# A long convolution and a token-mixing MLP on one core: zeros on TensorE ahead of the data, a third w2 buffer, a new order

## The chip, the cores and the metric

The kernel runs on one core of one Trainium2 chip. The metric is the device time of the whole program in microseconds, the median of several runs, lower is better. Five engines work side by side from their own instruction streams: TensorE (PE, matmul), VectorE (DVE), ScalarE (ACT), GpSimd (POOL) and SyncE (SP), which here only starts DMAs. They are tied together by semaphores.

## The reference, cut to what matters

There are S = 2048 tokens, D = 640 channels and F = 1536 hidden units, in bf16. The input `q` is also the input `x` of the second branch.

```python
def _A_ref(q, k, v, shift_k, ssm_k, ssm_D):        # causal long convolution
    k_shift[t] = sum_j k[t - j] * shift_k[:, j]     # 4 taps (written shorter here)
    kv = k_shift * v
    y = irfft(rfft(pad(kv, 2 * S)) * rfft(pad(ssm_k, 2 * S)))[:S].astype(bfloat16)
    y = y + kv * ssm_D
    return q * y

def _B_ref(x, w1, b1, w2, b2):                      # MLP over the tokens
    h = _layernorm(x)                               # over D
    u = gelu(einsum("bsd,sf->bdf", h, w1) + b1)
    return transpose(einsum("bdf,fs->bds", u, w2) + b2)

g = sigmoid((x * gate_w).sum(-1))
return g * a + (1 - g) * b
```

## The kernel before

**The convolution** is done in P = 4 blocks of 512 rows. A block of the filter `ssm_k` comes in as `wnat`, DVE folds it into sums and differences (`en`), the folds are transposed to `eo`, and TensorE multiplies `eo` by the tables `TFc` and `TFs` of cosines and sines, which gives the spectrum W. For blocks 0 and 1 the transposes are matmuls with the identity `idp`, and ACT copies them from PSUM to `eo`; for blocks 2 and 3 they are DMA transposes (`w_turn`, `w_freq`). A block of keys comes in transposed as `kT`, TensorE applies the 4 taps (`dg`), ACT copies the result to `ks`, a DMA transposes it to `kn`, DVE multiplies it by `vn` and folds it to `es` and `fs` (`kv_block`), and TensorE multiplies these by `AFc` and `AFs`; ACT writes the spectrum A (`a_freq`). DVE then forms the products of A and W block by block into `tT` and Z (`pair`), TensorE goes back with the table `TI` (`inverse`), and the `epilogue` takes `pb` and `qb` from PSUM on ACT, combines them in `cg` on DVE, multiplies them by the gated inputs `xe` and adds them to the output, mostly by accumulating DMAs of POOL. The last frequency needs its own small operation: the rows `nr0` to `nr3` are copied by four small DMAs into `WN`, a sum over neighbours gives `WN2`, and DVE multiplies it by `AN` into `ZN`.

**The MLP**: DVE makes the layernorm (`bn_stats`, then `h`), TensorE multiplies `h` by `w1` in groups of rows, ACT applies gelu into `gT`. Then `mlp2(q)` runs eight times: it loads 256 columns of `w2` (768 KB) and multiplies them in two groups of 24 matmuls of 320 columns, and ACT writes `o1`. The loads of w2 take turns in two buffers:

```python
        def w2_load(q):
            nm = f"w2_{q % 2}"
            dma(b[nm][:, :, :], dram(B_w2, q * 256, [[S, 128], [128 * S, FT], [1, 256]]), nm, 40.0 + q)
```

**What sets the order.** The program is first collected as a list of some 730 operations (`_Plan`). The tuple `ORDER` (lines 329 to 362) is a permutation of their numbers, and `plan.run(ORDER)` issues them in that order, each on its engine; so every engine's stream follows `ORDER`. A tracker adds a semaphore wait wherever an operation reads or overwrites what another engine or DMA produced. PSUM has four slots, given to the operations in the same order; buffers in SBUF are placed by their lifetimes. All DMAs but the gathering and accumulating ones are started by SP, in order, and a DMA that has to wait on SP holds those behind it.

**Names in the profile.** Each kind of operation is issued by one helper, so its line is the helper's: L310 matmul, L659 tensor-tensor, L666 and L667 tensor-scalar, L674 copy, L701 activation, L278 DMA, L265 DMA transpose, L269 to L273 POOL's DMAs, L677 memset, L884 and L886 layernorm statistics. Groups are told apart by the tile names.

Of the kernel before, what the change touches and what calls it, by code (L numbers as in the profile page):

```python
# [8 lines left out]
BF16 = mybir.dt.bfloat16  # L9
# [309 lines left out]
def bass_gated_mix__ssm_conv_h3__mixer_token_mlp__prompt_kernel(  # L319
# [7 lines left out]


ORDER = (
    12, 9, 13, 11, 14, 10, 21, 22, 155, 26, 15, 5, 0, 24, 23, 27, 1, 203, 28, 204, 16, 25, 31, 217, 32, 156, 205,  # L330
    206, 208, 160, 207, 154, 30, 209, 210, 332, 17, 18, 43, 44, 153, 211, 162, 166, 169, 40, 42, 41, 212, 213, 159,
    171, 38, 65, 161, 218, 214, 215, 216, 37, 58, 172, 219, 67, 33, 174, 36, 72, 6, 177, 59, 175, 170, 176, 220, 221,
    77, 29, 66, 3, 4, 73, 228, 34, 178, 35, 57, 2, 167, 68, 163, 164, 173, 232, 76, 229, 83, 74, 94, 75, 183, 78,
    116, 179, 105, 60, 168, 84, 39, 184, 61, 19, 20, 185, 180, 181, 234, 182, 107, 87, 88, 89, 106, 190, 233, 62,
    333, 95, 120, 138, 49, 150, 69, 109, 149, 151, 186, 235, 236, 99, 198, 191, 85, 192, 187, 63, 64, 199, 226, 227,
    127, 193, 335, 152, 86, 117, 118, 96, 200, 201, 97, 202, 79, 196, 121, 122, 80, 81, 98, 100, 197, 290, 108, 336,
    224, 82, 90, 194, 195, 188, 91, 119, 225, 230, 337, 70, 189, 71, 158, 132, 101, 231, 341, 92, 339, 342, 110, 340,
    279, 280, 281, 102, 222, 123, 103, 124, 104, 338, 343, 93, 140, 129, 334, 111, 112, 344, 282, 143, 223, 128, 130,
    139, 131, 133, 295, 142, 157, 46, 50, 113, 144, 45, 141, 114, 115, 47, 48, 283, 125, 126, 134, 135, 284, 136,
    285, 145, 137, 52, 54, 286, 146, 148, 259, 260, 147, 291, 287, 258, 409, 292, 408, 345, 346, 51, 53, 288, 289,  # L340
    407, 238, 237, 261, 239, 240, 352, 298, 356, 296, 357, 347, 353, 348, 349, 364, 360, 361, 297, 365, 562, 293,
    294, 7, 354, 355, 367, 358, 350, 359, 362, 363, 270, 351, 264, 265, 262, 268, 266, 263, 561, 271, 269, 274, 563,
    165, 243, 267, 368, 241, 244, 247, 242, 248, 245, 246, 253, 254, 564, 275, 276, 277, 272, 273, 423, 251, 252,
    413, 255, 256, 299, 366, 249, 250, 330, 331, 373, 257, 410, 278, 411, 374, 375, 369, 376, 371, 370, 429, 372,
    402, 404, 406, 303, 378, 401, 403, 405, 377, 412, 300, 304, 305, 56, 426, 590, 55, 427, 428, 430, 301, 560, 302,
    431, 414, 415, 591, 306, 565, 432, 379, 425, 380, 390, 381, 391, 383, 384, 385, 388, 389, 382, 392, 393, 592,
    396, 593, 418, 397, 596, 597, 307, 314, 433, 569, 398, 399, 567, 578, 566, 577, 579, 394, 386, 387, 311, 467,
    395, 416, 417, 598, 312, 313, 424, 580, 419, 420, 600, 568, 581, 469, 421, 308, 422, 309, 582, 434, 315, 319,
    310, 475, 599, 624, 322, 476, 625, 435, 626, 473, 471, 472, 400, 468, 474, 316, 317, 327, 436, 320, 457, 437,
    318, 458, 627, 323, 470, 594, 328, 628, 584, 459, 629, 460, 461, 478, 477, 329, 438, 446, 321, 442, 324, 447,  # L350
    325, 595, 440, 443, 326, 441, 452, 453, 454, 455, 603, 630, 479, 462, 614, 439, 481, 448, 449, 444, 445, 583,
    480, 486, 601, 487, 632, 631, 482, 463, 464, 602, 613, 604, 518, 465, 512, 466, 501, 636, 498, 499, 502, 503,
    450, 483, 519, 451, 504, 511, 505, 637, 456, 488, 506, 520, 638, 490, 572, 491, 605, 633, 616, 521, 615, 492,
    522, 570, 507, 575, 640, 493, 639, 508, 530, 515, 664, 571, 513, 665, 489, 634, 509, 573, 531, 524, 514, 8, 510,
    576, 500, 533, 574, 496, 532, 516, 666, 484, 485, 534, 525, 588, 606, 527, 667, 585, 517, 523, 542, 497, 668,
    635, 611, 608, 528, 607, 610, 543, 669, 617, 589, 609, 526, 670, 621, 612, 672, 671, 678, 535, 673, 545, 641,
    546, 587, 645, 618, 536, 529, 554, 656, 586, 674, 648, 647, 622, 675, 679, 494, 643, 654, 644, 677, 544, 547,
    623, 646, 676, 642, 653, 655, 537, 657, 682, 619, 539, 652, 650, 538, 658, 555, 683, 540, 495, 651, 548, 680,
    557, 684, 681, 686, 620, 556, 688, 541, 558, 702, 551, 552, 687, 649, 559, 705, 703, 685, 689, 690, 692, 693,
    659, 691, 694, 695, 661, 660, 697, 696, 708, 662, 698, 699, 709, 710, 700, 718, 549, 711, 717, 553, 707, 719,  # L360
    720, 713, 701, 704, 663, 712, 722, 714, 721, 550, 706, 715, 716, 723, 724, 725,
)


# [123 lines left out]
def _build(nc, A_q, A_k, A_v, A_shift_k, A_ssm_k, A_ssm_D, B_x, B_w1, B_b1, B_w2, B_b2, gate_w, out):  # L488
# [9 lines left out]
    FT = F // 128  # L498
# [5 lines left out]
    with ExitStack() as es:  # L504
# [15 lines left out]
        def buf(name, shape, dtype, t0, t1):  # L520
            spec.append((name, list(shape), dtype, t0, t1))

        END = 999
        buf("WN", [128, P + 1, 8], BF16, 0, END)
        buf("WN2", [128, P, 8], BF16, 0, END)
        buf("AN", [128, P, 8], BF16, 0, END)
        buf("ZN", [128, P, 8], BF16, 0, END)
        buf("PT", [128, P, 8], F32, 0, END)
        buf("gwc", [128, DC, 32], BF16, 0, 91)
# [7 lines left out]
        buf("nmr", [128, NT], F32, 0, 40)  # L537
        buf("gpre", [128, NT], F32, 0, END)
        buf("gth", [128, NT], F32, 0, END)
# [62 lines left out]
            buf(f"A{j}", [128, 2, NB, D], BF16, (50, 62, 82, 86)[j], END)  # L602
        for i in range(2):
            buf(f"Z{i}", [128, 2, NB, D], BF16, (62, 64)[i], END)
            buf(f"w2_{i}", [128, FT, 256], BF16, 91, END)
        NO = NT // 2
        WTD = (2, 3)
# [43 lines left out]
        def nel(ap):  # L651
            k = 1
            for st, ct in list(ap.ap)[1:]:
                k *= ct
            return k
# [20 lines left out]
        def memset(ap, val, pr, eng="POOL"):  # L676
            return vop(eng, 0.3 + nel(ap) / 2000.0, lambda e: e.memset(ap, val), [], [ap], pr)  # L677
# [40 lines left out]
        def pe(pslist, mms, pr, after=()):  # L718
            reads = []
            for m in mms:  # L720
                reads.append(m[3])
                reads.append(m[4])
            cost = sum(0.025 if len(m) == 8 else 0.035 if len(m) > 7 else max(0.1, 0.0235 + m[2] * 0.000375 + (0.02 if m[2] > 400 else 0))
                       for m in mms)

            def emit():
                full = []
                for m in mms:
                    ps_ = pp[m[0].slot]
                    if len(m) == 8:  # L730
                        o_ = ps_[m[7]:m[7] + 32, m[1]:m[1] + m[2]]
                    elif len(m) > 7:
                        q0, h0, z0 = m[7:]
                        o_ = ps_[q0:q0 + 64, h0:h0 + 512].rearrange("p (k z) -> p k z", k=2)[:, :, z0:z0 + 128]
                    else:
                        o_ = ps_[0:list(m[3].ap)[-1][1], m[1]:m[1] + m[2]]
                    full.append((o_,) + m[3:7])
                T.mm_part(full)

            return plan.add("PE", cost, emit, reads, [], pr, ps=pslist, after=after)  # L740
# [7 lines left out]
        def h2(ap):  # L748
            return ap.rearrange("p (c f) -> p c f", c=2)

        b = bufs
        cst = b["cst"]

        memset(cst[:, 0:1], float(np.float32(math.pi * (1.0 - 1e-6))), 0)
        memset(cst[:, 1:2], float(np.float32(-math.pi / 2)), 0)
# [106 lines left out]
        def w1t(s_, t):  # L862
            return b[f"w1_{(2 * s_ + t // 8) % 3}"][:, t % 8, :]
# [50 lines left out]
        p_ = _PS()  # L914
# [95 lines left out]
        for s_ in range(1, NSET):  # L1010
            w1_load(s_, 2.5 if s_ < 2 else 6.0 + 2 * s_)
            for fi in range(FSET):
                p_ = _PS(True)
                for hf in range(2):
                    pairs = [(w1t(s_, t)[:, fi * 128:(fi + 1) * 128], b["h"][:, t, :]) for t in range(8 * hf, 8 * hf + 8)]
# [147 lines left out]
                    dma(row5(Z, 7 * D), b["ZN"][:, m_, 0:5], f"zn{m_ % 2}", pr)  # L1163

        def w2_load(q):
            nm = f"w2_{q % 2}"
            dma(b[nm][:, :, :], dram(B_w2, q * 256, [[S, 128], [128 * S, FT], [1, 256]]), nm, 40.0 + q)

        def mlp2(q):
            w2_load(q)  # L1170
            for k in range(2):
                sb = 2 * q + k
                p_ = _PS()
                pairs = [(b[f"w2_{q % 2}"][:, ft, k * 128:(k + 1) * 128], b["gT"][:, ft, :]) for ft in range(FT)]
                pe([p_], halves(p_, pairs), 50.0 + q)
                act(h2(b[f"o1_{q}"][:, k, :]), two(p_), ACT.Identity, 3, bias=b["c2"][:, sb:sb + 1],
                    scale=b["omg"][:, sb:sb + 1], ps=[p_])
            if q < NO - 2:
                dma(rows(out, q), b[f"o1_{q}"][:, :, :], f"o1_{q}", 1.5)
            else:  # L1180
                dma(rows1(out, 2 * q + 1), b[f"o1_{q}"][:, 1, :], f"o1_{q}", 1.5)
# [103 lines left out]
        p_ = _PS()  # L1285
# [43 lines left out]
```

## Time and profile before

| | us |
|---|---|
| median of 3 runs | 190.94 (190.90 to 191.12) |
| the profiled execution's own time | 190.03 |
| span of the profile, first to last instruction | 188.0 |
| TensorE busy | 175.3 |
| DVE busy | 175.2 |
| ACT busy | 112.6 |
| POOL busy | 65.1 |

The span is 2.0 us shorter than the time of the same execution; the median of the runs is 0.91 us above that execution. Busy times of engines overlap, so they don't add up to the span; a group's mean is the duration of one record, and consecutive matmuls overlap, so that their pitch is shorter than a record.

### The profile page before, as it was taken

What the parts mean: (1) busy time and instruction counts of PE and PEld (TensorE: products, weight loads), DVE (VectorE), ACT (ScalarE), POOL (GpSimd) and SP (SyncE); (2) the same over time, 40 slices, a digit from 0 to 9 for tenths busy, and PEclk for the clock granted to TensorE, in tenths of its full rate; (3) what the DMA queues carried; (4) which work ended last, traced back from release to release, by engine and by line L of the source; (5) the groups of instructions that cost most, each with busy time, mean ns of one, the idle gap of its engine ahead of it and who ended that gap; (6) DMA issues with size and microseconds to landing.
All of it is one profiled execution on the core that took longest, in us unless ns stands there. A gap on an engine that the chain in (4) does not pass through costs nothing.

```text
span 188.0 us, 3972 instructions
## 1 busy us (share of the span) xinstructions
PE 175.3 (93%) x1636; PEld 124.1 (66%) x1636; DVE 175.2 (93%) x216; ACT 112.6 (60%) x173; POOL 65.1 (35%) x84
## 2 busy tenths in 40 slices
PE   0899999999999999999999999999999999996980
PEld 0566776766668766677776767677777777774750
DVE  6889999976999999999999999999999999999863
ACT  5989978439997079523420588453742845561781
POOL 7125587730000012000000000260068829988470
PEclk9999999999999999999999999999999999999997
DMA  5999989999999999994967892025688997598796
GB/s 164 315 266 277 338 235 247 228 125 201 289 232 231 193 233 228 257 242 119 247 190 145 185 277 73 2 71 170 168 246 274 209 247 229 107 185 241 128 148 130
DMA packets 78094, 38.04 MB, mean 202 GB/s; under 512 B 42492, under 2 KB 77564, under 8 KB 78076
## 3 DMA queue, kind: packets, MB, share of 16 engines
q1 hardware_dynamic: 75340, 32.87, 70.9%
q0 software_dynamic: 2736, 4.92, 14.3%
q8 instruction: 13, 0.21, 0.4%
q14 instruction: 5, 0.04, 0.1%
HBM read 23.08 MB, written 4.92 MB: 149 GB/s over the span
## 4 chain that ended last, share of the span: by engine, by line
PE 89%; DMA 7%; DVE 1%; ACT 0%; ACTq 0%; SPq 0%; issue 0%
PE pp L310 89%; DMA w<-in_B_w_dram 4%; DMA wnat<-in_A_ssm_k_dram 2%; DVE cg L659 1%; ACT o L701 0%; ACTq L322 0%; DVE en L659 0%; SPq L278 0%
## 5 line engine op out<-in xcount | busy, mean ns | idle before, releaser
L310 PE MATMUL pp<-gT,w 128*128 128x320 bf16 x384 | 53.4, 299 | 1.6 <-DMA w<-in_B_w_dram 1.6
L310 PE MATMUL pp<-h,w 128*128 128x320 bf16 x384 | 54.2, 299 | 0.1
L310 PEld LDWEIGHTS pp<-gT,w 128*128 128x128 bf16 x384 | 37.4, 98 | 16.4 <-DMA w<-in_B_w_dram 1.9
L659 DVE TENSOR_TENSOR tT<-A,W 128x5120 bf16<-128x5120 bf16 (+2 forms) x18 | 45.5, 2525 | 2.8 <-ACT A L701 2.6
L310 PEld LDWEIGHTS pp<-h,w 128*128 128x128 bf16 x384 | 36.9, 98 | 15.5 <-issue 1.3
L659 DVE TENSOR_TENSOR Z<-Z,tT 128x2560 bf16<-128x2560 bf16 (+5 forms) x29 | 46.4, 1625 | 0.1
L271 POOL DMA_INDIRECT xe<-in_A_q_dram,bidx x8 | 20.6, 2575 | 66.3 <-PE pp L310 48.7
L701 ACT ACTIVATE o<-pp,c,omg 128x640 bf16<-128x640 f32 x16 | 13.9, 881 | 21.7 <-PE pp L310 21.7
L701 ACT ACTIVATE A<-pp 128x640 bf16<-128x640 f32 x32 | 20.7, 712 | 7.8 <-PE pp L310 7.7
L271 POOL DMA_INDIRECT vn<-in_A_v_dram,bidx x8 | 9.4, 1170 | 32.5 <-DVE kn L659 31.4
L701 ACT ACTIVATE gT<-pp,bf 128x640 bf16<-128x640 f32 x12 | 9.3, 793 | 16.6 <-PE pp L310 16.6
L310 PE MATMUL pp<-Z,TI 128*128 128x320 bf16 x128 | 18.9, 299 | 0.0
L269 POOL DMA_INDIRECT out_dram<-cg,bidx x8 | 15.5, 1936 | 2.9 <-issue 1.8
L701 ACT ACTIVATE W<-pp 128x640 bf16<-128x640 f32 x24 | 15.6, 759 | 1.0 <-PE pp L310 1.0
L310 PEld LDWEIGHTS pp<-Z,TI 128*128 128x128 bf16 x128 | 12.2, 98 | 5.2 <-ACT o L701 0.2
L884 DVE BATCH_NORM_STATS2 stats<-xs 128x6 f32<-128x320 bf16 x32 | 13.8, 471 | 0.1
L310 PE MATMUL pp<-eo,TFc 128*128 128x320 bf16 x64 | 12.6, 321 | 0.0
L701 ACT ACTIVATE ks<-pp 128x1024 bf16<-128x1024 f32 (+1 forms) x12 | 10.1, 892 | 3.6 <-PE pp L310 3.6
L659 DVE TENSOR_TENSOR Z<-A,W 128x5120 bf16<-128x5120 bf16 x4 | 11.3, 2822 | 0.5 <-ACT A L701 0.5
L310 PE MATMUL pp<-eo,TFs 128*128 128x320 bf16 x64 | 10.5, 300 | 0.0
L310 PE MATMUL pp<-idp,en 128*128 128x128 bf16 x40 | 4.7, 287 | 5.6 <-DVE par_i L666 4.7
L310 PE MATMUL pp<-kT,dg 64*64 64x256 bf16 x320 | 9.8, 270 | 0.0
(100 smaller groups left out, 207.5 us busy)
## 6 DMA issues: line engine op xcount, KB each, us to landing
w<-in_B_w_dram SPq DMA_DIRECT2D x8, 768.0 KB, 5.8
w<-in_B_w_dram SPq DMA_DIRECT2D x10, 512.0 KB, 4.7
xs<-in_A_q_dram SPq DMA_DIRECT2D x7, 320.0 KB, 5.1
out_dram<-o SPq DMA_DIRECT2D x6, 320.0 KB, 4.8
vn<-in_A_v_dram SPq DMA_DIRECT2D x4, 320.0 KB, 3.8
wnat<-in_A_ssm_k_dram SPq DMA_DIRECT2D x2, 640.0 KB, 6.2
xe<-in_A_q_dram SPq DMA_DIRECT2D x4, 320.0 KB, 3.1
w<-in_B_w_dram SPq DMA_DIRECT2D x4, 256.0 KB, 5.2
```

The lines of the kernel that those rows point to most:

```text
L269: ins = engobj.indirect_dma_start(whole, off, in_ap, None, compute_op=ALU.add)
L271: ins = engobj.indirect_dma_start(out_ap, None, whole, off)
L310: ins = self.nc.tensor.matmul(ps_ap, lhsT=lhsT, rhs=rhs, start=start, stop=stop)
L659: return vop(eng, c, lambda e: e.tensor_tensor(out_, in0, in1, op), [in0, in1], [out_], pr)
L701: return e.activation(out_, src, func, **kw)
L884: vop("DVE", 0.41, (lambda o_, i_: lambda e: e.bn_stats(o_, i_))(o_, i_), [i_], [o_], pr)
```

## The change

- A buffer `warm` of 128 x 512 is added, a DVE memset fills it with zeros, and as its first work TensorE multiplies 128 x 128 of it with 128 x 512 of it, eight times, into a PSUM slot that nothing reads. It waits only for the memset.
- The loads of w2 take turns in three buffers, no longer two.
- `ORDER` is written anew (the numbers of all operations rise by two through the added ones, and a great many change places).

Otherwise the operations are the same ones: TensorE has 1644 matmuls for 1636, DVE has one more instruction.

```diff
 ORDER = (
-    12, 9, 13, 11, 14, 10, 21, 22, 155, 26, 15, 5, 0, 24, 23, 27, 1, 203, 28, 204, 16, 25, 31, 217, 32, 156, 205,
...
+    14, 158, 11, 16, 33, 34, 0, 12, 13, 15, 1, 23, 24, 19, 2, 26, 163, 28, 29, 157, 74, 7, 208, 162, 161, 3, 207, 25,
...
         END = 999
+        buf("warm", [128, 512], BF16, 0, 7)
         buf("WN", [128, P + 1, 8], BF16, 0, END)
...
         for i in range(2):
             buf(f"Z{i}", [128, 2, NB, D], BF16, (62, 64)[i], END)
+        for i in range(3):
             buf(f"w2_{i}", [128, FT, 256], BF16, 91, END)
...
         cst = b["cst"]
+
+        memset(b["warm"][:, :], 0.0, 0, eng="DVE")
+        p_ = _PS()
+        pe([p_], [(p_, 0, 512, b["warm"][:, 0:128], b["warm"][:, :], True, True)] * 8, -9.0)
...
         def w2_load(q):
-            nm = f"w2_{q % 2}"
+            nm = f"w2_{q % 3}"
...
-                pairs = [(b[f"w2_{q % 2}"][:, ft, k * 128:(k + 1) * 128], b["gT"][:, ft, :]) for ft in range(FT)]
+                pairs = [(b[f"w2_{q % 3}"][:, ft, k * 128:(k + 1) * 128], b["gT"][:, ft, :]) for ft in range(FT)]
```

Where the new order matters for the steps below: on DVE the memset is the third instruction; up to the second `fs` DVE has the same operations as before, one table operation on `AFs` moved behind them; on SP the four small copies `WN<-nr` leave in the order nr3, nr2, (`AN`), nr1, with nr0 earlier, and the second direct load of `vn` follows the two `kn` transposes; the eight loads of w2 use the buffers 1, 0, 2, 0, 1, 2, 0, 1, and all but the first stand behind the copies `AN<-A` of block 2 and `Z1<-ZN`; both scalings of the last `xe0` come before the last `o` on ACT.

## The prediction, made before the changed kernel was run

> **What bounds the kernel now.** I began with the busy row and the chain of waits on the page. Two engines are almost full: TensorE (PE) and VectorE (DVE) both work 93% of the span, and the chain that ended last runs 89% on TensorE.
>
> ```profile
> PE 175.3 (93%) x1636; PEld 124.1 (66%) x1636; DVE 175.2 (93%) x216; ACT 112.6 (60%) x173; POOL 65.1 (35%) x84
> PE 89%; DMA 7%; DVE 1%; ACT 0%; ACTq 0%; SPq 0%; issue 0%
> ```
>
> The chain in order of time (start, length, what) then shows where TensorE is not the link: the first load of `wnat`, one load of `w2` late in the run, and the output.
>
> ```profile
> 1.25 4.30 DMA wnat<-in_A_ssm_k_dram
> ...
> 77.07 86.31 PE pp L310 x751
> 163.40 8.01 DMA w<-in_B_w_dram
> 171.45 11.05 PE pp L310 x80
> 182.53 0.89 ACT o L701
> ```
>
> TensorE's timeline (start, length, instruction, count, idle time before and its releaser) gives both ends of this:
>
> ```profile
> 6.20 2.87 PE L310 MATMUL pp<-idp,en 128*128 128x128 bf16 x23 [0.93 <-DVE en L659]
> 8.88 1.78 PE L310 MATMUL pp<-eo,TFc 128*128 128x320 bf16 x6
> ...
> 14.64 1.53 PE L310 MATMUL pp<-eo,TFc 128*128 128x320 bf16 x10
> ...
> 139.02 13.20 PE L310 MATMUL pp<-gT,w 128*128 128x320 bf16 x96
> ...
> 171.45 3.43 PE L310 MATMUL pp<-gT,w 128*128 128x320 bf16 x24 [1.57 <-DMA w<-in_B_w_dram]
> 174.72 4.51 PE L310 MATMUL pp<-Z,TI 128*128 128x320 bf16 x32
> 179.07 3.42 PE L310 MATMUL pp<-gT,w 128*128 128x320 bf16 x24
> ```
>
> At 8.88 six matmuls of 320 columns need 1.78 us, a pitch of (1.78 - 0.47) / 5 = 0.26 us, where 0.47 is the record of a single one there. At 139.02 the pitch is 13.20 / 96 = 0.136. So TensorE runs at half speed at the start, and the records turn short (0.30 a matmul) at 12.2 us, 6.0 us after it became continuously busy at 6.20. The page's clock row shows full speed throughout the opening; the durations decide here. Priced at the later pitch, the work of 6.2 to 12.2 takes about 3.0 us, so the slow start costs TensorE 3.0 us. The other loss is the 1.57 us on `w2`: that load waits for its buffer until 163.40 and lands 8.0 us later, while the 48 matmuls of the other buffer cover 48 x 0.136 = 6.5.
>
> DVE's timeline says how much of these 4.6 us can come through:
>
> ```profile
> 39.56 1.56 DVE L659 TENSOR_TENSOR fs<-es 128x1280 bf16<-128x1280 bf16 x2
> 43.76 2.83 DVE L659 TENSOR_TENSOR tT<-A,W 128x5120 bf16<-128x5120 bf16 x1 [2.63 <-ACT A L701]
> 47.12 2.83 DVE L659 TENSOR_TENSOR Z<-A,W 128x5120 bf16<-128x5120 bf16 x1 [0.54 <-ACT A L701]
> ...
> 61.70 0.17 DVE L659 TENSOR_TENSOR WN<-WN 128x20 bf16<-128x20 bf16 x1
> ...
> 175.44 0.90 DVE L659 TENSOR_TENSOR Z<-Z,tT 128x640 bf16<-128x640 bf16 x2
> ```
>
> From 47.12 to 176.3 DVE has no gap: 20.00 of 20 us in each stretch. The last Z ends at 176.34, and behind it lie 16 matmuls of Z and 24 of `gT`, 40 x 0.136 = 5.4 us; DVE alone therefore allows TensorE's end at 181.8, against 182.4 now. Saving on TensorE alone is worth 0.6 us at most. Anything more has to bring DVE's unbroken run forward.
>
> **The change, part by part.** *The zeros.* They add one DVE memset of 128x512 (estimate 0.15 to 0.3 us, the small DVE rows of 0.15 and the 0.43 of an idx operation on as many elements) and eight matmuls of 512 columns. At the cold pitch these take 8 x 0.26 x 512/320 = 3.4 us. DVE is idle to 1.20, so they run from about 1.8 to 5.2. The first real operands came at 4.67 (four transposes) and 6.20; the new order brings the first at about 6.05. TensorE idles there today, so the zeros cost nothing; if they ended later than 6.05, every us late would count in full. If they raise the clock by 6, the 3.0 us vanish from TensorE. They don't turn into 3.0 of lead: ACT is busy from 6.74 to 26.08 with five gaps, 2.3 us in all, and so paces the PSUM slots, and the stages behind need DVE's folds and `h`.
>
> *DVE's lead.* Up to the second `fs`, DVE runs the same 100 instructions in both orders, with the memset in place of one 0.15 us operation. Before, they hold 41.12 us, of which 1.20 + 0.38 + 0.21 + 0.69 + 0.68 = 3.16 are idle. The first 1.20 waits for POOL and stays; the 0.38 is filled by the memset; 0.69 waits for `wnat` and 0.68 for `bf`, which comes through TensorE and can come sooner. I take 2.1 us idle after: `fs` ends at about 40.1, a lead of 1.0 (0.4 if nothing but the small gaps goes, 1.6 if the two long ones nearly go). From `fs` the path is the same as today's: two matmul groups, `A` on ACT, `tT`. DVE's Z at 47.12 moves to about 46.05, lead 1.07.
>
> *The order around WN.* The four `WN<-nr` copies feed one 0.17 us DVE operation; everything on DVE stands behind it. Before, the last pair left SP at 57.21 to 58.35 and DVE used it at 61.70 without waiting, so the second landed in at most 3.9. The new order puts that last copy third in a row of small ones, after an `AN<-A`, leaving SP at about 57.65 (estimate). The nearest row for its landing is that `AN<-A` copy, 4.2 us, in a stretch where the DMA share was 1.13. DVE, 1.1 early, is there at 60.6: the stall is between 0 (landing in 2.9) and 1.3 (4.2). I take 0.5. The second `vn` load goes behind the `kn` transposes on SP: issued about 62.2, landing 3.8 as the group's median says, at 66.0, when DVE wants it at 65.95; 0 to 0.5, and I take 0.
>
> *Three w2 buffers.* The same eight loads; the third buffer lets each start one load earlier. In the new order 76 to 108 matmuls lie between a buffer's release and its next use, 10.3 to 14.7 us against 8.0 for the slowest landing seen. The 1.57 goes; what is late next is DVE's Z. All loads but the first now wait on SP behind `AN<-A` and `Z1<-ZN`; they have 6 us to spare by my reading, so 0. Should a load again find only 6.5 us of cover, 1.5 returns.
>
> *The tail.* Both scalings of the last `xe` now stand before the last `o` on ACT, so after TensorE's end there are 0.9 (`o`), 0.5 (`cg`) and the output, where today a scaling and two additions more follow (182.53 to 185.18). The last POOL accumulation, 182.22 today and ending the span 5.8 later, needs DVE's `cg` and moves only with DVE.
>
> *Sum.* By TensorE alone: 182.43 - 1.57 - about 1.0 = 179.9. By DVE: 181.8 - 1.07 + 0.5 = 181.2, and this is the later. Then 0.1 + 0.9 + 0.5 brings `cg` to 182.75; from the last `cg` to the end is 188.0 - 185.18 = 2.8 today, so 185.55. The last accumulation: its `cg` follows DVE's Z by about the same time as today, less 1.6 from earlier scalings and the lead; about 180.6 + 5.8 = 186.4, the later end. The span falls from 188.0 to about 186.3, hence the profiled time from 190.03 to about 188.3. The median of the runs stands 0.91 above that profiled time: 189.2. With every unknown at its ends (lead 0.4 to 1.6, stall 0 to 1.3) the case gives 188.1 to 190.0.
>
> **A rule beside the row.** Row: the clock rose 6.0 us after 6.20, although 6.2 to 8.9 was busy with short transposes. The Trainium skill ("TensorE: Matmul & The Clock Gate", Part 1) says that the clock doubles after one busy window of about 3.4 us, and that the windows run freely. By that rule zeros of 3.4 us rarely fill a whole window, and a gap behind them spoils the next; the first full window would end 3.4 to 6.8 us after 6.05, between 9.5 and 12.9, which is the first rival below. No row of this profile has a busy run of 3.4 us followed by a gap, so no number here depends on the rule, and nothing here excludes it.
>
> **Rivals.** *The clock stays low until about 12.* For: the transposes' stretch, three quarters busy, did not raise it, and a gap of 0.85 follows the zeros. Against: TensorE is busy far earlier than today. Then there is no lead; WN is waited for by nobody; the `w2` stall alone goes, and DVE's 181.8 holds: 0.6 from TensorE, and up to 0.7 more from the tail. Median 189.7 to 190.5, about 190.1. Chance 0.18.
>
> *All of it comes through.* No WN stall, a lead of 1.4 to 1.6: 187.4 to 188.1. Chance 0.09.
>
> *The gain goes elsewhere, or the change does not do what it says.* The lead is eaten by several 0.3 us waits on DVE, and `w2` still stalls: 190.56 to 191.3. Chance 0.07.
>
> *Slower: the WN copies land late.* They leave SP right among loads of `w1` and `kT`, and the page gives 4.7 for such a `w1` load, the trace 6.3 for the `kT` transposes and 8.0 for one `w2` load. One DVE instruction waits for all four, with the whole of DVE's unbroken run behind it. At a landing of 8.0 after 57.65, DVE goes on at 65.65 and not 60.6: a stall of 5.0, less the 0.5 counted, 189.2 + 4.5 = 193.7. At 6.3, 3.3 of stall, 192.0. It turns slower when the stall passes 2.6, a landing past 5.5. Against: today's copies needed at most 3.9 in the same stretch. Chance 0.19, most of it at 191.4 to 193.
>
> **How the numbers follow.** The main case has 0.47. About 0.2% of the time, 0.38 us, is what a measurement of this kernel tells from no change. Faster: 0.47 + 0.09 + 0.17 of the late clock = 0.73. Same: 0.07 + 0.01 = 0.08. Slower: 0.19. The range 187.6 to 191.9 takes in the main case, the late clock, half of the full gain and the mild third of the slow case, and leaves out about 0.17. The likeliest case's own range is 188.1 to 190.0.
>
> **What would show it.** Right: TensorE's 320-column records at 0.30 before 9 us; `fs` ending near 40.1 and the first long `tT` starting near 42.7; a wait of up to 1.3 at DVE's `WN` near 60.6; no `w2` wait in TensorE's row; the last Z ending near 175.8 and TensorE near 181.2. Wrong: records of 0.47 as late as today's 12 us (late clock); `tT` no earlier than 43.76; a gap on DVE over 2.6 us after 47; or a TensorE wait for `w2` left at the end.

## The result: slower by 1.5%, and the profile after

The changed kernel takes 193.94 us (median of 6 runs, 193.28 to 194.36) against 191.03 for the kernel before in the same comparison (190.29 to 191.56): ratio 1.0154, 95% interval 1.0127 to 1.0181. Its profiled execution took 193.96 us with a span of 192.1. The prediction was 189.2 with a range up to 191.9.

The page of the changed kernel, busy row and chain:

```profile
PE 180.0 (94%) x1644; PEld 125.2 (65%) x1644; DVE 175.6 (91%) x217; ACT 112.0 (58%) x173; POOL 69.6 (36%) x84
DVE 52%; PE 14%; ACT 10%; POOL 7%; DMA 7%; SPq 4%; issue 3%; DVEq 0%
```

The chain has left TensorE for most of the span: up to 157.5 us it now runs over DVE, ACT, POOL and a DMA, and only its last part (23.7 us from 157.47 on) lies on TensorE. TensorE's 180.0 holds the zeros (3.6) and a second stretch at half clock, below. Next, what DVE waited for (total us, times, longest):

```profile
DVE cg L661 <- ACT xe L703: 3.3, 1, 3.3
DVE tT L661 <- ACT A L703: 2.0, 1, 2.0
DVE en L661 <- DMA wnat<-in_A_ssm_k_dram: 1.5, 3, 0.6
DVE Z L661 <- ACT A L703: 1.4, 1, 1.4
```

The first line is new. DVE's timeline shows where it stands:

```profile
39.55 1.56 DVE L661 TENSOR_TENSOR fs<-es 128x1280 bf16<-128x1280 bf16 x2
43.21 2.83 DVE L661 TENSOR_TENSOR tT<-A,W 128x5120 bf16<-128x5120 bf16 x1 [2.04 <-ACT A L703]
47.44 2.83 DVE L661 TENSOR_TENSOR Z<-A,W 128x5120 bf16<-128x5120 bf16 x1 [1.40 <-ACT A L703]
62.02 0.17 DVE L661 TENSOR_TENSOR WN<-WN 128x20 bf16<-128x20 bf16 x1
150.63 2.82 DVE L661 TENSOR_TENSOR tT<-A,W 128x5120 bf16<-128x5120 bf16 x1
156.77 0.82 DVE L661 TENSOR_TENSOR cg<-cg,xe 128x1280 bf16<-128x1280 bf16 x1 [3.32 <-ACT xe L703]
179.03 0.89 DVE L661 TENSOR_TENSOR Z<-Z,tT 128x640 bf16<-128x640 bf16 x2
```

Up to 150.63 DVE is 0.3 us later than before (its `tT` stood at 150.32 there). Then it stands still for 3.3 us, because `cg` needs the scaled `xe`, and is 3.7 later from there on; the last Z ends at 179.92 and not at 176.34. So 0.3 + 3.3 makes 3.6 of the 4.1 us by which the span grew; the other 0.5 lies behind the last Z (12.2 us to the end, 11.7 before). In the kernel before, the same two operations follow without a break:

```profile
150.32 2.83 DVE L659 TENSOR_TENSOR tT<-A,W 128x5120 bf16<-128x5120 bf16 x1
153.06 0.82 DVE L659 TENSOR_TENSOR cg<-cg,xe 128x1280 bf16<-128x1280 bf16 x1
```

Why `xe` is late stands on POOL's timeline (DMA_INDIRECT `xe` is a gather, `out_dram` an accumulation). First the changed kernel, then the kernel before:

```profile
135.27 8.25 POOL L269 DMA_INDIRECT out_dram<-cg,bidx  x1 [9.33 <-DVE cg L661]
143.82 2.44 POOL L269 DMA_INDIRECT out_dram<-cg,bidx  x1 [0.30 <-issue]
146.56 1.99 POOL L271 DMA_INDIRECT xe<-in_A_q_dram,bidx  x1 [0.30 <-issue]
148.86 1.20 POOL L271 DMA_INDIRECT xe<-in_A_q_dram,bidx  x1 [0.30 <-issue]
```

```profile
137.95 3.29 POOL L271 DMA_INDIRECT xe<-in_A_q_dram,bidx  x1 [12.28 <-DVE cg L659]
141.55 2.55 POOL L271 DMA_INDIRECT xe<-in_A_q_dram,bidx  x1 [0.30 <-issue]
144.09 1.41 POOL L273 DMA_DIRECT2D out_dram<-cg  x1
145.81 2.49 POOL L269 DMA_INDIRECT out_dram<-cg,bidx  x1 [0.30 <-issue]
```

Before, the two gathers of the next block's `xe1` went out first and the accumulations of the block behind them. The new order has it the other way round, and the first accumulation holds POOL for 8.25 us; the second gather starts 7.3 us later than before (148.86 for 141.55) and its rows reach ACT only at 155.9. ACT, in order, then holds `pb` and `qb` too, and with them a PSUM slot, so TensorE waits as well:

```profile
1.96 3.60 PE L310 MATMUL pp<-warm 128*128 128x512 bf16 x8 [1.96 <-DVE warm L679]
6.37 2.31 PE L310 MATMUL pp<-idp,en 128*128 128x128 bf16 x20 [0.81 <-DVE en L661]
157.47 5.10 PE L310 MATMUL pp<-gT,w 128*128 128x320 bf16 x24 [2.52 <-ACT pb L703]
```

The wait for `w2` is gone from TensorE's rows, but in its place stands this one of 2.52 us. Behind it 24 matmuls take 5.10 us, where 3.42 is the rule: the granted clock was halved from 157.6 to 161.1. That cost nothing that the runs show. A fall of 3.4 us to half clock takes 0.009 off the mean granted clock of a run; two of the six runs, with a mean of 0.996 and 0.997, can therefore have had none, and they took 193.93 and 193.84, like the rest.

### The profile page after: what moved, and what is told of

Same layout as the page of the kernel before. It is cut to its first block, busy times and chain, and to the rows that moved or that the text cites. A ratio compares the mean times of both kernels' runs of the same rounds, so it can differ in the third digit from the quotient of the medians.

```text
span 192.1 us, 3987 instructions
## 1 busy us (share of the span) xinstructions
PE 180.0 (94%) x1644; PEld 125.2 (65%) x1644; DVE 175.6 (91%) x217; ACT 112.0 (58%) x173; POOL 69.6 (36%) x84
## 4 chain that ended last, share of the span: by engine, by line
DVE 52%; PE 14%; ACT 10%; POOL 7%; DMA 7%; SPq 4%; issue 3%; DVEq 0%
DVE Z L661 16%; PE pp L310 14%; DVE tT L661 11%; POOL out_dram L269 6%; DVE stats L890 5%; ACT W L703 5%; DMA xe<-in_A_q_dram,bidx 4%; DVE es L661 3%; DVE fs L661 3%; DVE kn L661 3%; DVE cg L661 3%; DMA wnat<-in_A_ssm_k_dram 3%; DVE h L669 2%; SPq L278 2%; DVE en L661 2%
## 5 line engine op out<-in xcount | busy, mean ns | idle before, releaser
L310 PE MATMUL pp<-gT,w 128*128 128x320 bf16 x384 | 55.1, 305 | 2.5 <-ACT pb L703 2.5
L310 PE MATMUL pp<-h,w 128*128 128x320 bf16 x384 | 54.8, 299 | 0.0
L310 PEld LDWEIGHTS pp<-gT,w 128*128 128x128 bf16 x384 | 38.0, 99 | 18.5 <-issue 3.0
L271 POOL DMA_INDIRECT xe<-in_A_q_dram,bidx x8 | 17.7, 2209 | 57.1 <-PE pp L310 49.2
L269 POOL DMA_INDIRECT out_dram<-cg,bidx x8 | 22.0, 2756 | 11.8 <-DVE cg L661 10.3
L271 POOL DMA_INDIRECT vn<-in_A_v_dram,bidx x8 | 8.7, 1089 | 32.6 <-DVE kn L661 30.4
L310 PEld LDWEIGHTS pp<-Z,TI 128*128 128x128 bf16 x128 | 12.3, 98 | 5.1 <-issue 0.2
L310 PE MATMUL pp<-kT,dg 64*64 64x256 bf16 x320 | 10.4, 271 | 0.0
L703 ACT ACTIVATE xe<-xe,ggr 128x640 bf16<-128x640 bf16 x8 | 6.5, 825 | 6.5 <-DMA xe<-in_A_q_dram,bidx 6.4
```

The costliest lines, as they stand in the source:

```text
L269: ins = engobj.indirect_dma_start(whole, off, in_ap, None, compute_op=ALU.add)
L271: ins = engobj.indirect_dma_start(out_ap, None, whole, off)
L310: ins = self.nc.tensor.matmul(ps_ap, lhsT=lhsT, rhs=rhs, start=start, stop=stop)
L703: return e.activation(out_, src, func, **kw)
```

## The experiments

All ratios are to the kernel before, timed beside it on the same chip; three chips were used, on which the kernel before took 189.4 to 190.1. "Last Z" is the end of DVE's last Z in the profile.

**1. The gathers go first again.** The changed kernel, two operations moved on POOL:

```diff
-        plan.run(ORDER)
+        order = list(ORDER)
+        for k in (609, 610):                      # the gathers of xe1
+            order.remove(k)
+            order.insert(order.index(589), k)     # ahead of the first accumulation
+        plan.run(order)
```

> The changed kernel with one thing moved: on POOL the two gathers of xe1 for the next block go ahead of the two indirect accumulations of the block before. Theory 1 (the gain went into a late xe1 on POOL's queue: DVE waits 3.3 us for it at one cg): that wait goes, DVE's last Z ends near 176.7 and the median is about 190.6 (190.0 to 191.2), the same as before or a little under. Theory 2 (the zeros, the clock that falls again after 157 us, or the third buffer's loads cost the time): still 193 to 194.5. Theory 3 (an accumulation on POOL is slow in itself, 8.2 us wherever it stands): the wait moves to a later cg and the median is 192 to 194.

190.82 us, ratio 1.0126 (1.0071 to 1.0181, 4 runs), too wide to decide on, but the profile does: DVE's wait for `xe` is gone from its list, last Z ends at 176.22, the span is 187.6. Theory 3 is half right: POOL's slow turn has passed on to the gather.

```profile
134.95 7.57 POOL L271 DMA_INDIRECT xe<-in_A_q_dram,bidx  x1 [9.32 <-DVE cg L661]
142.83 2.50 POOL L271 DMA_INDIRECT xe<-in_A_q_dram,bidx  x1 [0.31 <-issue]
```

Whatever stands first at 135 takes about 8 us, yet both gathers are out by 145.3 and nobody waits. So it was run again beside the changed kernel, with more runs of each:

> The changed kernel again, unchanged, beside the others of this call on one chip. All theories: 1.5 to 2.5 % above the kernel before, with DVE's wait of 3.3 us at the cg that multiplies by xe, and an accumulation on POOL of about 8 us at 135 us.

> The changed kernel with the two gathers of xe1 ahead of the accumulations on POOL, a second time with more runs. Theory 1 (POOL's queue is the whole loss): within 0.4 % of the kernel before and 1.3 to 2 % under the changed kernel. Rival (a second loss in the new order that the one profile does not show): 0.8 to 1.5 % above the kernel before.

The changed kernel: 193.56 us, ratio 1.0161 (1.0117 to 1.0205), with DVE's wait of 3.0 us at that `cg`. With the gathers first: 191.31 us, ratio 1.0057 (1.0027 to 1.0088). POOL's order alone is therefore about 1.0% of the 1.6%; some 0.6% is left, and theory 1 in its strict form (the whole loss) falls.

**2. The same swap in the kernel before**: accumulations 587 and 586 ahead of the gathers 608 and 607.

```diff
+        for k in (587, 586):
+            order.remove(k)
+            order.insert(order.index(608), k)
```

> The kernel before with one thing moved: on POOL the two indirect accumulations of block 1 go ahead of the two gathers of xe1 for the next block, the order of the changed kernel. Theory 1: the wait appears here too, DVE idles 2 to 4 us at the cg that multiplies by xe, median 193 to 195. Theory 2 (zeros, clock or third buffer): 191.0 as before, within 0.5.

192.0 us, ratio 1.014 (1.0052 to 1.0229); DVE waits 2.4 us for `xe` at the same `cg`, and its last Z ends at 178.94. The loss appears in the old order too, without zeros or a third buffer. It appears even without the 8 us on POOL:

```profile
140.56 1.63 POOL L269 DMA_INDIRECT out_dram<-cg,bidx  x1 [14.73 <-DVE tT L659]
142.50 2.37 POOL L269 DMA_INDIRECT out_dram<-cg,bidx  x1 [0.31 <-issue]
148.09 1.79 POOL L271 DMA_INDIRECT xe<-in_A_q_dram,bidx  x1 [0.30 <-issue]
```

Here the accumulations are short, but the first starts only at 140.56, when DVE's `tT` has ended, and the second gather starts 6.5 us later than in the kernel before (148.09 for 141.55). The accumulations' place ahead of the gathers is what the two cases have in common.

**3. No zeros.** The changed kernel without the memset and its eight matmuls.

> The changed kernel without the memset and the eight matmuls of zeros, everything else as it is. Theory 1 (POOL's queue): nothing of the 3.3 us wait changes, median 193.5 to 194.3; the accumulation of 8.2 us and the wait of DVE for xe are there again. Theory 2 (the zeros themselves cost): 191 to 192.5. If the clock rises later than the 10.9 us of the changed kernel, the zeros did raise it by that much.

194.04 us, ratio 1.0294 (1.024 to 1.0347), on the chip on which the kernel before took 189.4. The 8.25 us accumulation and a DVE wait of 2.9 us are there again, last Z ends at 179.99 (179.92 with zeros). The clock rose at 10.93 us, with zeros at 10.87. The zeros neither caused the loss nor gained anything that these two profiles show; this kernel and the changed one were not timed side by side, so a difference of some tenths of a percent stays open.

**4. Why 8 us on POOL.** In the changed kernel DVE runs five long bf16 operations on SBUF operands without a break between 134.9 and 141.9, then a small one, `PT<-PT` (to 142.07), and POOL's accumulation ends at 143.52, 1.4 us behind that. The small one, 128x5, was moved in among the long ones, nothing else:

```diff
+        order = list(ORDER)
+        order.remove(636)                         # PT<-PT
+        order.insert(order.index(590), 636)       # ahead of the cg at 137.7
+        plan.run(order)
```

> The changed kernel with one small DVE operation moved: PT<-PT, 128x5, goes from behind the cg at 141.2 to before the cg at 137.7. Theory A (POOL's indirect DMA can end only after a small DVE operation stands between DVE's long ones): the accumulation that starts at 135.3 ends near 139 instead of 143.5, xe comes 4 us earlier, DVE's wait of 3.3 us goes and the median is 190 to 191. Theory B (it is held by something else, DMA traffic or its own code): it still ends near 143.5, median as the changed kernel.

POOL's and DVE's timelines of this run:

```profile
134.96 4.05 POOL L269 DMA_INDIRECT out_dram<-cg,bidx  x1 [9.33 <-DVE cg L661]
139.32 6.64 POOL L269 DMA_INDIRECT out_dram<-cg,bidx  x1 [0.30 <-issue]
```

```profile
137.39 0.17 DVE L661 TENSOR_TENSOR PT<-PT 128x5 f32<-128x5 f32 x1
144.43 0.15 DVE L661 TENSOR_TENSOR ZN<-PT 128x5 bf16<-128x5 f32 x1
```

The accumulation now ends at 139.01, 1.4 us after the small operation, as theory A said. But the next accumulation then has no small operation to end by until `ZN` at 144.43, and takes 6.64: it ends at 145.96, 1.4 us behind that one. The gathers start only 0.3 us earlier than in the changed kernel, and the time stays at 193.27 us, ratio 1.0161 (1.0112 to 1.021); in this profile, of the quickest of the five runs (192.07), DVE's wait at the `cg` is 1.9 us. So it is shown that the moved DVE operation sets when POOL's accumulation ends here, and the forecast of the time missed, since I had asked only about the first of the two accumulations.

As a general rule theory A does not hold. In the kernel before DVE runs only long operations of the same kinds from 140.49 to 150.20, and meanwhile a gather ends at 144.10 after 2.55 us and an accumulation at 148.30 after 2.49; the 1.63 and 2.37 of experiment 2 end beside such operations too. Why POOL's first DMA at 135 is held for about 8 us in the new order, and none for so long in the old, stays open.

The Trainium skill describes this in "SBUF — State Buffer": GpSimd and VectorE share a pair of SBUF ports as a lock ("Who interferes with whom"), and a DMA issued on GpSimd has its descriptors written by that engine, so it can wait on VectorE ("SBUF: two separate sides"). The 8.25 that turned into 4.05 agrees with a wait on VectorE; that it outlasts five operations is not explained by this. The page adds that tensor-tensor did not stall such DMAs in its own probe; here all the operations in the way are tensor-tensor, and the measurement decides. What in the small operation opens the way (its type, its size, or something else) is not shown.

**5. What the w2 wait was worth.** The kernel before, the load of the seventh group cut to a twelfth:

```diff
-            dma(b[nm][:, :, :], dram(B_w2, q * 256, [[S, 128], [128 * S, FT], [1, 256]]), nm, 40.0 + q)
+            nf = 1 if q == 6 else FT
+            dma(b[nm][:, 0:nf, :], dram(B_w2, q * 256, [[S, 128], [128 * S, nf], [1, 256]]), nm, 40.0 + q)
```

> The kernel before, whose load of w2 for the seventh group (the one that TensorE waits 1.57 us for) fetches only the first of its twelve parts, 64 KB instead of 768; the output of that group is made with old weights. DVE theory (DVE's unbroken run sets the end): the 1.57 us wait goes, TensorE ends at 181.8 at the earliest, and the median falls by 0.3 to 0.8, to about 190.4. TensorE theory (the wait is on the path in full): it falls by 1.5, to 189.4. Hidden altogether: 191.0.

189.02 us, ratio 1.0003 (0.9972 to 1.0034). TensorE no longer waits for `w2`; it waits 0.80 us for DVE's Z instead, and the time does not move: -0.5 to +0.6 us, which excludes the TensorE theory's 1.5 and leaves room only for the low end of the DVE theory's 0.3 to 0.8. The third buffer alone was not run, so what it is worth by itself is not shown.

**6. What an early clock is worth.** The kernel before with a memset as DVE's first instruction and thirteen matmuls of zeros, so that almost no gap is left ahead of the data; its order is otherwise the old one.

```diff
+        buf("warm", [128, 512], BF16, 0, 7)
...
+        memset(b["warm"][:, :], 0.0, 0, eng="DVE")
+        p_ = _PS()
+        pe([p_], [(p_, 0, 512, b["warm"][:, 0:128], b["warm"][:, :], True, True)] * 13, -9.0)
...
-        plan.run(ORDER)
+        plan.run([0, 1] + [k + 2 for k in ORDER])
```

> The kernel before with the memset and thirteen matmuls of zeros first on DVE and TensorE (0.5 to about 6.1 us if all run cold), its order otherwise untouched, so that hardly a gap is left before the first data at 6.2. If zeros without a gap raise the clock: 320-column records of 0.30 from 9 us on or earlier, no half-speed stretch, TensorE ahead by 1.5 to 3 us at 12. Prediction's step (an early clock gives DVE a lead of 0.4 to 1.6): tT starts at 42.2 to 43.4 instead of 43.76, median 0.3 to 1.3 us under before. Rival (ACT and DVE set the opening): tT at 43.5 or later, median as before within 0.3.

```profile
38.46 1.56 DVE L660 TENSOR_TENSOR fs<-es 128x1280 bf16<-128x1280 bf16 x2
42.65 2.83 DVE L660 TENSOR_TENSOR tT<-A,W 128x5120 bf16<-128x5120 bf16 x1 [2.63 <-ACT A L702]
```

The clock rose at 5.35 us, and DVE's lead is there: `fs` ends at 40.02 (41.13 before), `tT` starts at 42.65 (43.76). The lead does not all arrive: 189.5 us, ratio 0.9974 (0.9946 to 1.0002), and timed a second time:

> The kernel before with thirteen matmuls of zeros, unchanged from the run before, for a closer interval. Theory 1 (an early clock gives DVE about 0.8 us of lead in the old order, most of which reaches the end): 0.2 to 0.5 % under before. Rival: no difference, 0.1 % either way.

189.58 us, ratio 0.9988 (0.9957 to 1.0019); in that profile `fs` ended at 40.98 although the clock rose at 5.41. Each interval alone includes no change.

Then the changed kernel, gathers first, with the same early zeros:

```diff
-        pe([p_], [(p_, 0, 512, b["warm"][:, 0:128], b["warm"][:, :], True, True)] * 8, -9.0)
+        pe([p_], [(p_, 0, 512, b["warm"][:, 0:128], b["warm"][:, :], True, True)] * 13, -9.0)
...
+        order = [0, 1] + [k for k in ORDER if k > 1]
+        for k in (609, 610):
+            order.remove(k)
+            order.insert(order.index(589), k)
+        plan.run(order)
```

> The changed kernel with the gathers ahead of the accumulations, the memset moved to be DVE's first instruction and thirteen matmuls of zeros for eight, so that the clock is up by about 5.5 us as a rule. Theory 1 (in the new order the opening waits for wnat and DVE, and an early clock gives nothing): fs still ends at 40.7 to 41.2 and the median is 0.2 to 0.7 % above before. Rival (the late clock is why the new order lost its lead): fs ends near 40, median 0 to 0.6 % under before.

190.83 us, ratio 1.0054 (1.0025 to 1.0083), as without them. DVE's timeline:

```profile
10.51 1.36 DVE L661 TENSOR_TENSOR en<-wnat 128x512 bf16<-128x512 bf16 x3 [0.66 <-DMA wnat<-in_A_ssm_k_dram]
39.74 1.56 DVE L661 TENSOR_TENSOR fs<-es 128x1280 bf16<-128x1280 bf16 x2
```

`fs` ends at 41.30. The new order puts an `xs` and rows of `brow` ahead of the second `wnat` block: in the changed kernel its two loads leave SP at 3.95 and 5.38 (2.28 to 3.2 before), and DVE begins to fold it at 10.0 to 10.6 in the profiles of the new order, where the old order without zeros did so at 7.5 to 8.1. Over all profiles, with the time at which the granted clock rose:

| | clock up at, us | second `fs` ends at, us |
|---|---|---|
| old order, no zeros (3 profiles) | 11.4 to 12.0 | 40.8 to 41.3 |
| old order, 13 early zeros (4) | 4.1 to 5.5 | 39.7 to 41.0 |
| new order, 8, 13 or no zeros (7) | 4.9 to 10.9 | 40.7 to 41.4 |

In the old order an early clock moves `fs` by 0.9 on average, by 0.1 to 1.4 in the single profiles; in the new order `fs` ends no earlier with the clock up at 4.9 than at 10.9.

**7. A version from this.** The old order, the thirteen zeros, and ACT's order around the first A changed, so that the two tiles that `tT` waits for don't stand behind `gT`. In the second kernel TensorE also makes the rest of A ahead of the next group of `h`:

```diff
+        order = list(ORDER)
+        for k in (297, 365):                      # gT, then the A tile that is made first
+            order.remove(k)
+            order.insert(order.index(361), k)
+        for k in (351, 293, 294):                 # only in the second kernel
+            order.remove(k)
+            order.insert(order.index(270), k)
+        plan.run([0, 1] + [k + 2 for k in order])
```

The first kernel changes only ACT's order; in what was expected of it, "the one before" is the second kernel, told behind it.

> As the one before, but only ACT's order around the first A is changed, TensorE's is not: tT near 42.0 as there, but Z still waits until 45.5 to 46.0 for the rest of A, so that nothing is gained over the kernel with zeros alone: 0.2 to 0.5 % under before. Rival: 0.6 to 0.8 % under it.

189.24 us, ratio 0.9972 (0.9946 to 0.9997): the only one whose interval lies under 1, by so little that one of several such kernels can do so by chance. That it is quicker than the kernel with zeros alone (0.9988 beside it) is not shown. Then the second kernel:

> The kernel before with thirteen matmuls of zeros, and around the first spectrum A: ACT writes gT ahead of the two A tiles that tT waits for and these in the order in which TensorE makes them, and TensorE does the rest of A ahead of the next sixteen matmuls of h. DVE's two waits for A (2.6 and 0.5 us) should shrink by 0.6 and by 0.5: tT near 42.0, Z following without a wait. Theory 1 (DVE's unbroken run sets the end): 0.6 to 1.1 % under before. Rival (ACT's chain of W behind it is as tight and DVE waits there instead): as the kernel with zeros alone.

189.93 us, ratio 0.9993 (0.9966 to 1.0019). `tT` starts at 41.65 and Z follows at 44.39 without a wait, 2.7 us ahead of the old kernel. Then it is the rival's case:

```profile
51.79 4.54 DVE L660 TENSOR_TENSOR W<-W,W 128x2560 bf16<-128x2560 bf16 x3 [1.66 <-ACT W L702]
```

ACT's chain of W is behind DVE by now, takes back 1.66, and the last Z ends at 176.19.

## Why the prediction was wrong, by its own steps

- **What bounds the kernel.** Right: DVE's unbroken run sets the end. Taking away TensorE's 1.57 us (experiment 5) brought nothing that can be measured.
- **DVE's run stays unbroken to the last Z.** This is the step that failed. The working went through SP's queue for WN, `vn` and `w2`, and looked at POOL only in the tail ("moves only with DVE"). POOL's queue between 120 and 160 was never walked, though `ORDER` had exchanged gathers and accumulations there. It costs 3.3 us on DVE and about 1% of the time. Even walked at the rows of before (2.49 and 1.71 for the accumulations) it would have shown the gathers later by 2.49 + 1.71 + 0.6 = 4.8 us, with scaled rows that stood ready 3.5 us ahead of need (149.56 on ACT for a `cg` at 153.06): a wait of about 1.3 us. Experiment 2, with short accumulations in that place, shows 2.4. The 8.25 was in no row.
- **DVE's lead of 1.0.** Wrong for this kernel: the second `fs` ends at 41.11 for 41.13. The idle time up to there is 1.20 + 0.52 + 0.62 + 0.33 + 0.26 = 2.93, not the 2.1 that I took: the waits for `wnat` grew with the new order of loads, whatever the clock did. In the old order the term is right in size (a mean of 0.9).
- **From `fs` the path is the same as today's.** Not quite: `tT` and Z wait 2.04 + 1.40 for A, 0.27 more than 2.63 + 0.54, and Z starts 0.32 later than before.
- **WN.** No stall, where 0.5 was counted. The last copy left SP at 59.30 to 59.86, 1.7 us later than estimated, and DVE used it at 62.02 straight behind its work: it landed in 2.7 us or less. The `vn` load and the loads of w2 made nobody wait, as forecast. The slower rival, which had its place here, had the right form (one DVE operation with everything behind it, waiting for a late DMA) and the wrong place.
- **The zeros.** Right that they cost nothing: they end at 5.56, the data come at 6.37. Whether they raise the clock before 6 us differs from one execution to the next: with the same eight matmuls, ending at 5.3 to 5.6, it rose at 4.94, 6.13, 7.03, 8.00 and 10.87. Two of these show the two ends: 20 transposes took 2.31 us in the profile above, and in the second profile of the same kernel 1.60:

```profile
5.89 1.60 PE L310 MATMUL pp<-idp,en 128*128 128x128 bf16 x20 [0.57 <-DVE en L661]
```

 The spread has a pattern. In each of the 14 profiles all changes of the granted clock lie whole multiples of 3.413 us apart (in the changed kernel 43, then 1, then 8 of them), and where this grid lies against the start differs from one execution to the next. By its records TensorE is busy for 83% or more of the 3.413 us that end at the first rise, and for 77% or less of the 3.413 us before them. So the zeros raise the clock when enough of them fall into one step of the grid, gap included, and this is left to chance with 3.6 us of them. The rule of the Trainium skill that the prediction weighed ("TensorE: Matmul & The Clock Gate", Part 1, a free-running window of about 3.4 us) agrees with such a grid. The prediction's working of it, in which a gap spoils a window and the rise comes between 9.5 and 12.9, does not: four of the five rises came earlier.
- **The tail.** No gain: from TensorE's end to the span's end it is 6.1 us (5.5 before). The last accumulation starts at 185.73 and sets the end, 6.3 us later; that both are tied to DVE's Z was right. (TensorE's end before is 182.49 in its row, 179.07 + 3.42, where the sum has 182.43; this changes nothing in it.)
- **What stays open.** With POOL mended, 0.5 to 0.6% remain (1 us). The first Z starts at 47.1 to 47.7 in its three profiles and at 46.8 to 47.3 in the three of the old order without zeros, which explains some 0.4 us of it; between the first Z and the last the mended kernel (129.1 to 129.3 us) is no slower than the old one (129.2). The rest would have to lie in the tail, where the profiles differ by 1 us from one to the next (from the last Z to the end 11.4 to 12.3 us in the three of the mended kernel, 11.1 to 11.7 in the three of the old order), and is not settled. The third buffer was in no run by itself, so its part in this is open too.

## What to carry to other kernels

When an order is rewritten, walk every queue in order, the one of the engine that is hardly busy too: POOL worked 35% of the time and set the loss, since a DMA that nobody waits for yet stood ahead of one that the busiest engine was about to need. If two engines are both full, an improvement on one is worth at most its distance to the other; find that distance first, and follow the engine that has none. A matmul of zeros ahead of the data was free here, but worth only what the engines behind TensorE could take up.

## What the runs showed of the hardware

- A DMA that POOL prepares can be held by DVE: the same accumulation took 8.25 us and, with one small DVE operation put among the long ones, 4.05, ending 1.4 us behind it. It is not always held: beside long DVE operations of the same kinds, accumulations of the old order took 1.63 to 2.49 us.
- The clock fell again after a gap of 2.1 to 2.5 us on TensorE (three profiles) for 3.41 us each time. TensorE was busy for 26 to 40% of the 3.413 us that ended at the fall; where it was busy for more than half of such a step of the grid, the clock stayed up in all profiles. The Trainium skill ("TensorE: Matmul & The Clock Gate", the section on oscillation) speaks of gaps of over 3.4 us; here a shorter one was enough. By their mean clock other executions of the same kernel had no such fall.
